# A RetNet recurrence and a PReLU feed-forward block in one kernel: the second half of w_out loaded as fp32 by SyncE's queue and cast on chip, and unit 3 turned by a transposing DMA transfer

## The chip, the cores and the metric

The kernel runs on one core of a Trainium2 chip. The metric is the device time of one launch in microseconds (us). Five engines work beside each other, each in the order of its own list of instructions: TensorE (PE in the profile, with its weight loads as PEld), VectorE (DVE), ScalarE (ACT), GpSimd (POOL) and SyncE (SP, SPq for its DMA queue). Semaphores join them. DMA transfers are issued by SyncE, ScalarE or GpSimd.

## The reference

```python
def _attn_ref(q, k, v):                       # q, k, v: 4 x 8 x 768 x 64
    gamma = 1.0 - 2.0 ** (-5.0 - np.arange(H))
    for t in range(S):
        state = gamma * state + einsum('bhd,bhe->bhde', k[:, :, t], v[:, :, t])
        y[:, :, t] = scale * einsum('bhd,bhde->bhe', q[:, :, t], state)

def _moe_ref(x, w_in, w_out, alpha):          # 3072 x 512, 512 x 2048, 2048 x 512
    h = x @ w_in
    g = np.maximum(h, 0.0) + alpha * np.minimum(h, 0.0)
    return g @ w_out
```

The recurrence's y, with its heads side by side, is x of the second function. All inputs and the output are fp32; the kernel multiplies in fp16 and sums in fp32.

## The kernel before

Each of the four sequences is cut into three units of 256 tokens, so there are units 0 to 11, and two units make a block of 512 tokens for the feed-forward part: blocks 0 to 5. The recurrence is computed in chunks: per unit, scores of q against k under a mask, times v, plus q times the state that is carried on.

For each unit the program does the following. `load` brings k, q and v as fp32 by SyncE's queue (L165, and L159 from unit 4 on, where k and v come in four pieces each); the tiles are ks, qs and vs, with three buffers of each. `rescale` (L185) multiplies k and q by powers of gamma into the fp16 tile kdq; `cast_v` (L201) makes the fp16 tile vx. Then kdq has to be turned, 16 blocks of 128x128, into kq, which has the head dimension on the partitions. For units 0 to 3 `turn_pe` does that on TensorE in two calls of eight transposes into a PSUM bank (trb, L230), each followed by a copy on ScalarE (kq<-trb, L236). From unit 4 on `turn_dma` (L205) does it in one transposing DMA transfer from SBUF to SBUF. `score_mm` (sca and scb, L466) reads kq, `masks` follows on VectorE, `sum_mm` (st, L260) sums the state from kdq and vx, `state_sum` and `state_copy` carry it on, `out_mm` (y, L501, L515 and L533) makes the unit's output, and `take_y` (xT, L556) brings it to SBUF in fp16.

The feed-forward part of a block is `ffn1` (hps, L632; the PReLU with hm on ScalarE, L648, and gt on VectorE, L650) and then the product with w_out: `ffn2` for block 0 (ops, L809, evicted by ScalarE, L819), and from block 1 on `ffn2_seven`, which forms seven products where eight would be needed, from sums of quarters of g and of w_out (ox, oy, L857). The sums of w_out's quarters, wsum, are made once by `w_sums` (L572): the first on GpSimd from w_out's first half alone, three on VectorE, which read the second half too.

The order of everything is written out by hand. `ffn1` and `ffn2` are generators; `tick(gen, m)` puts the next m matmuls of one into TensorE's list, so that the unit's small products stand between them. Around unit 3, `gen` is `ffn2` of block 0 (64 matmuls of 512 columns, in four groups of 16; a group reads four of w_out's 16 row tiles), and `half` is `ffn1` of block 1, of which 48 matmuls need only unit 2. The banks in which these 48 are summed are given by a list, six turns of eight matmuls.

Weights are brought as fp32 and cast to fp16 on chip: `get_wo32(i)` loads part i of w_out, two row tiles (512 KB), into space that is free early, and `cast_wo` casts it on the engine that is given. That holds for parts 0 to 3. The second half comes by `get_wo` (L982), a DMA transfer that GpSimd issues and that casts on its way, in two transfers of four row tiles. The second piece of the loads of unit 4, its q, waits for the first of these two, by `held`.

SyncE's queue is one list: a transfer whose condition isn't met stands in the way of all behind it.

Of the kernel before, what the change touches and what calls it, by code (L numbers as in the profile page):

```python
# [9 lines left out]
FP = mybir.dt.float32  # L10
# [12 lines left out]
def kernel(  # L23
# [10 lines left out]
    nc = tc.nc  # L34
    B, H, S, D = q.shape
# [41 lines left out]
    sbp = ctx.enter_context(tc.tile_pool(name="sbp", bufs=1, space=bass.MemoryType.SB))  # L77
# [38 lines left out]
    held, late, last_g = [], [], []  # L116
# [26 lines left out]
    def load(u, parts="kqv"):  # L143
        if u >= NU:
            return
        b, c = divmod(u, UPB)
        t = staged.setdefault(u, {})
        for nm in parts:
            src = {"k": k, "q": q, "v": v}[nm[0]]
            if nm[0] not in t:  # L150
                t[nm[0]] = sbp.tile(
                    [128, H, 2 * D], FP, tag=f"{nm[0]}s", bufs=3, name=f"{nm[0]}s{u}"
                )
            h = slice(0, H) if len(nm) == 1 else slice(4 * int(nm[1]), 4 * int(nm[1]) + 4)
            if u >= SPLIT and nm != "q":
                for x in range(2):
                    for y in range(2):
                        at = U * c + 128 * x + 64 * y
                        nc.sync.dma_start(  # L159
                            out=t[nm][rows(x), :, D * y : D * y + D],  # L160
                            in_=src[b, :, at : at + 64, :].rearrange("h p d -> p h d"),
                        )
                continue
            hold(
                nc.sync.dma_start(  # L165
                    out=t[nm[0]][:, h, :],
                    in_=src[b, h, U * c : U * c + U, :].rearrange(
                        "h (p r) d -> p h (r d)", r=2
                    ),
                )  # L170
            )
# [10 lines left out]
    def rescale(eng, u, t, h0, h1):  # L182
        kdq = unit(u)[0]
        at = OQ if t else (O2 if u >= SPLIT else 0)
        return eng.tensor_tensor(  # L185
            out=kdq[:, t, :, h0:h1, :].rearrange("p r h d -> p h r d"),
            in0=staged[u]["kq"[t]][:, h0:h1, :].rearrange("p h (r d) -> p h r d", r=2),
            in1=tab[:, at + 2 * h0 : at + 2 * h1]
            .rearrange("p (h r) -> p h r", r=2)
            .unsqueeze(3)  # L190
            .to_broadcast([128, h1 - h0, 2, D]),
            op=MULT,
        )

    def cast_v(eng, u, h0=0, h1=H):
        o = unit(u)[2][:, h0:h1].rearrange("p h r d -> p (h r d)")
        i = staged[u]["v"][:, h0:h1].rearrange("p h x -> p (h x)")
        if eng is nc.scalar:
            eng.activation(out=o, in_=i, func=COPY, bias=0.0, scale=1.0)
        else:  # L200
            eng.tensor_copy(out=o, in_=i)  # L201

    def turn_dma(u):
        kdq, kq, _ = unit(u)
        nc.sync.dma_start_transpose(out=kq, in_=kdq.rearrange("p t r h d -> p (t r h d)"))  # L205
# [410 lines left out]
    def ffn1(n, banks, apart=0):  # L616


        turns = [(f, 2, ul, ul + 1) for ul in range(2) for f in range(0, apart, 2)]
        rest = range(apart, NFT)  # L620
        if apart == 0:
            rest = [f + x for f in range(HF) for x in (0, HF)]
        turns += [(f, 1, 0, 2) for f in rest]
        gt = None
        for i, (f0, nf, lo, hi) in enumerate(turns):
            hps = ps(banks[i % len(banks)], "hps").rearrange("p (f t) -> p f t", f=nf)
            parts = [(f, lo, hi) for f in range(nf)]
            if n > 1 and i == 0:
                parts = [(0, 0, 1), (0, 1, 2)]
            for f, ul, uh in parts:  # L630
                for hp in range(4):
                    nc.tensor.matmul(  # L632
                        out=hps[:, f, U * (ul - lo) : U * (uh - lo)].rearrange(
                            "p (u t) -> p u t", t=U
                        ),
                        lhsT=w_in_all[:, hp, 128 * (f0 + f) : 128 * (f0 + f) + 128],
                        rhs=xT[n][:, ul:uh, hp, :],
                        start=(hp == 0),
                        stop=(hp == 3),
                    )  # L640
                    if (f, ul, uh) != parts[-1] or hp < 3:
                        yield
            if gt is None:
                gt = sbp.tile([128, NFT, TB], F16, tag="gt", bufs=2, name=f"gt{n}")
                gts[n] = gt
            hm = sbp.tile([128, TB], FP, tag="hm", bufs=3, name="hm")
            hm = hm.rearrange("p (f t) -> p f t", f=nf)
            nc.scalar.activation(out=hm, in_=hps, func=RELU, bias=0.0, scale=-1.0)  # L648
            for f in range(nf):
                nc.vector.scalar_tensor_tensor(  # L650
                    out=gt[:, f0 + f, U * lo : U * hi],
                    in0=hm[:, f, :],
                    scalar=oma_sb[:, f0 + f : f0 + f + 1],
                    in1=hps[:, f, :],
                    op0=MULT,
                    op1=ADD,
                )
            if n > 0 and f0 in ((HF + 3, NFT - 1) if apart == 0 else (NFT - 1,)):

                lo = 0 if apart or f0 < NFT - 1 else 4  # L660
                hi = HF if f0 == NFT - 1 else 4
                g_sums(n, 0, lo, hi)
                g_sums(n, 1, lo, hi)
            yield
# [294 lines left out]
    def tick(gen, m=10**6):  # L959
        for _ in range(m):  # L960
            if next(gen, 1) == 1:
                return
# [14 lines left out]
            return eng.activation(out=o, in_=i, func=COPY, bias=0.0, scale=1.0)  # L977
        return eng.tensor_copy(out=o, in_=i)  # L978

    def get_wo(i):  # L980
        s = slice(4 * i, 4 * i + 4)
        return nc.gpsimd.dma_start(out=w_out_all[:, s, :], in_=wo[:, s, :])  # L982

    def wo_part(i):
        return early[i // 2][:, 1, 2 * (i % 2) : 2 * (i % 2) + 2, :]

    def get_wo32(i):
        nc.sync.dma_start(out=wo_part(i), in_=wo[:, 2 * i : 2 * i + 2, :])
# [113 lines left out]
    rescale(G, 2, 1, 4, 8)  # L1102
    cast_wo(G, 3)
    load(3, ("k", "q", "v"))
    cast_v(G, 2)
    out_mm(1, (4, 5), evict=False)
    take_y(1, (0,))
# [2 lines left out]


    gen = ffn2(0, (0, 1, 2, 3), parts=4)
    half = ffn1(1, (6, 7, 4, 5, 4, 6, 0, 1, 2, 3, 0, 4, 5, 6, 7, 1), apart=12)
    tick(gen, 8)
    turn_pe(2, 0, 5)
    tick(gen, 6)
# [7 lines left out]
    sum_mm(2, (5, 4))  # L1124
    state(2, 0, G, "ga")
    masks(2, 1)
    held.append(get_wo(2))
    load(4)
    load(5)
    rescale(G, 3, 0, 0, 8)  # L1130
    rescale(G, 3, 1, 0, 8)
    get_wo(3)
    cast_v(G, 3)
    w_sums(0, 0, HF, G)
    tick(gen, 7)
    out_mm(2, (4, 5))
    tick(gen, 6)
    tick(half, 24)
    turn_pe(3, 0, 6)
    tick(half, 8)  # L1140
    turn_pe(3, 1, 7)
    tick(half, 16)
    tick(gen, 9)
    score_mm(3, 0, (4, 5))
    masks(3, 0)
# [192 lines left out]
```

## Time and profile before

| | us |
|---|---|
| median of 3 runs | 198.63 (198.36 to 198.85) |
| the profiled execution | 198.86 |
| its span | 196.9 |
| TensorE busy in the span | 189.3 |
| VectorE, ScalarE, GpSimd busy | 156.3, 115.4, 106.1 |

The span runs from the first to the last instruction of the profiled execution, and the profile's times count from its start. The chain of work that ended last is followed back from the last instruction, at each step to what released it. A row of the timeline has start, length, engine, line, operation and tiles, and in brackets the idle time ahead of it and what ended it. A group's row has its busy time and the mean of one in ns. The granted clock of TensorE was 0.997 of full speed over the span.

### The profile page before, as it was taken

The numbers are of one execution on the slowest core, as the hardware profiler recorded it, in microseconds if no ns is written. First come the engines' busy times: TensorE is split into PE (matmuls) and PEld (weight loads), VectorE is DVE, ScalarE is ACT, GpSimd is POOL, SyncE is SP. The second block draws the span as 40 slices with busy tenths as digits, with TensorE's granted clock in tenths as the row PEclk, the third lists the DMA queues.
The fourth block names the chain that finished last, engine by engine and source line by source line (L and its number), as shares of the span: only waits on it lengthen the run. The fifth ranks groups of instructions, "written<-read, shape, count | busy, mean of one in ns | idle before, by whom it ended". The sixth has DMA issues, their size and how long they took to land.

```text
span 196.9 us, 6085 instructions
## 1 busy us (share of the span) xinstructions
PE 189.3 (96%) x2529; PEld 128.8 (65%) x2529; DVE 156.3 (79%) x259; ACT 115.4 (59%) x199; POOL 106.1 (54%) x113
## 2 busy tenths in 40 slices
PE   6688999999999999999999999999999999999993
PEld 2356645568467688744688744788644788865882
DVE  7698987517698998289988389977489996999983
ACT  4458665349187668467467476467466486678110
POOL 3176897499549544970077980076970180039300
PEclk9999999999999999999999999999999999999998
DMA  5999999998879989898988899929865010400014
GB/s 156 313 317 380 374 381 377 293 180 136 211 192 200 286 197 265 213 311 175 213 203 209 256 201 191 222 65 225 256 122 126 17 57 3 160 3 0 0 65 152
DMA packets 90026, 37.92 MB, mean 193 GB/s; under 512 B 57984, under 2 KB 87696, under 8 KB 90000
## 3 DMA queue, kind: packets, MB, share of 16 engines
q1 hardware_dynamic: 88768, 36.45, 69.2%
q0 software_dynamic: 1056, 1.05, 3.6%
q8 instruction: 20, 0.33, 0.6%
q10 hardware_dynamic: 176, 0.04, 0.1%
q14 instruction: 6, 0.05, 0.1%
HBM read 27.31 MB, written 6.29 MB: 171 GB/s over the span
## 4 chain that ended last, share of the span: by engine, by line
PE 90%; SPq 4%; DMA 3%; DVE 0%; issue 0%; POOL 0%; DVEq 0%
PE hps L632 36%; PE ox L857 16%; PE oy L857 12%; PE ops L809 7%; SPq L165 4%; PE hps L719 4%; PE sp L761 3%; DMA vs<-in_v_dram 3%; PE y L533 1%; PE y L384 1%; PE trb L230 1%; PE st L284 1%; PE sca L466 1%; PE ov L857 1%; PE ow L857 1%; PE oz L857 1%
## 5 line engine op out<-in xcount | busy, mean ns | idle before, releaser
L632 PE MATMUL hps<-xT,win 128*128 128x512 f16 (+1 forms) x396 | 71.5, 338 | 0.3 <-DVE ss L423 0.3
L650 DVE SCALAR_TENSOR_TENSOR gt<-hm,oma,hps 128x512 f16<-128x512 f32 (+1 forms) x96 | 59.4, 656 | 12.1 <-issue 4.3
L648 ACT ACTIVATE hm<-hps 128x512 f32<-128x512 f32 x80 | 47.6, 597 | 24.6 <-PE hps L632 22.5
L632 PEld LDWEIGHTS <-win 128*128 128x128 f16 x396 | 38.1, 98 | 31.0 <-POOL win L978 0.4
L857 PEld LDWEIGHTS <-gs 128*128 128x128 f16 x320 | 31.0, 98 | 3.7
L857 PEld LDWEIGHTS <-gt 128*128 128x128 f16 x240 | 22.9, 98 | 4.0
L333 POOL CAST tg<-tm 64x256 f16<-64x256 f32 x12 | 4.8, 396 | 34.3 <-DVE tm L301 22.3
L185 POOL TENSOR_TENSOR kdq<-qs,tab 128x1024 f16<-128x1024 f32 (+1 forms) x12 | 20.2, 1686 | 3.0 <-DVE wsum L572 2.3
L185 POOL TENSOR_TENSOR kdq<-ks,tab 128x1024 f16<-128x1024 f32 (+1 forms) x12 | 20.2, 1686 | 2.6 <-PE y L515 2.6
L857 PE MATMUL ox<-wout,gt 128*128 128x256 f16 x144 | 17.3, 273 | 0.0
L857 PE MATMUL oy<-wsum,gs 128*128 128x256 f16 x144 | 17.2, 273 | 0.0
L556 ACT ACTIVATE xT<-y 128x512 f16<-128x512 f32 x22 | 14.9, 744 | 3.1 <-PE y L533 2.0
L201 POOL CAST vx<-vs 128x1024 f16<-128x1024 f32 (+1 forms) x13 | 12.6, 970 | 6.7 <-DMA vs<-in_v_dram 6.7
L809 PE MATMUL ops<-wout,gt 128*128 128x512 f16 x64 | 15.3, 380 | 0.0
L613 DVE TENSOR_TENSOR gs<-gt 128x1024 f16<-128x1024 f16 (+1 forms) x14 | 13.0, 934 | 0.2
L877 ACT ACTIVATE cu<-oy 128x512 f32<-128x512 f32 x10 | 6.0, 597 | 10.6 <-PE oy L857 10.1
L236 ACT ACTIVATE kq<-trb 128x1024 f16<-128x1024 f16 x8 | 8.2, 1023 | 6.3 <-PE trb L230 6.3
L313 POOL TENSOR_TENSOR tf<-ss,tab 128x256 f32<-128x256 f32 x10 | 10.3, 1028 | 2.5 <-DVE ss L312 1.3
L881 DVE TENSOR_TENSOR os<-ox,cu 128x512 f32<-128x512 f32 x5 | 3.4, 687 | 10.1 <-PE ox L857 10.1
L670 POOL TENSOR_SCALAR hn<-qc,oma 128x256 f32<-128x256 f32 x4 | 4.5, 1138 | 12.4 <-DVE qc L785 12.3
L809 PEld LDWEIGHTS <-gt 128*128 128x128 f16 x64 | 5.8, 98 | 6.0
L424 POOL TENSOR_TENSOR tf<-ss,tab 128x256 f32<-128x256 f32 x6 | 5.9, 980 | 7.1 <-DVE ss L423 7.1
(119 smaller groups left out, 293.1 us busy)
## 6 DMA issues: line engine op xcount, KB each, us to landing
qs<-in_q_dram SPq DMA_DIRECT2D x9, 512.0 KB, 5.4
ks<-in_k_dram SPq DMA_DIRECT2D x32, 128.0 KB, 3.5
vs<-in_v_dram SPq DMA_DIRECT2D x32, 128.0 KB, 4.6
early<-in_moe_w_in_dram SPq DMA_DIRECT2D x7, 512.0 KB, 7.5
out_dram<-os SPq DMA_DIRECT2D x9, 256.0 KB, 2.5
early<-in_moe_w_out_dram SPq DMA_DIRECT2D x4, 512.0 KB, 7.0
out_dram<-ot SPq DMA_DIRECT2D x4, 512.0 KB, 3.8
ks<-in_k_dram SPq DMA_DIRECT2D x6, 256.0 KB, 6.1
```

What stands on the lines that cost most here:

```text
L165: nc.sync.dma_start(out=t[nm[0]][:, h, :], in_=src[b, h, U * c : U * c + U, :].rearrange("h (p r) d -> p h (r d)", r=2),)
L185: return eng.tensor_tensor(out=kdq[:, t, :, h0:h1, :].rearrange("p r h d -> p h r d"), in0=staged[u]["kq"[t]][:, h0:h1, :].rearrange("p h ...
L201: eng.tensor_copy(out=o, in_=i)
L236: nc.scalar.activation(out=kq.rearrange("p (x a) i -> p x a i", x=4)[:, :, 2 * hh : 2 * hh + 2, :], in_=trb.rearrange("p (x a i) -> p x a ...
L313: nc.gpsimd.tensor_tensor(out=t, in0=ss, in1=dec, op=MULT)
L556: nc.scalar.activation(out=o, in_=i, func=COPY, bias=0.0, scale=1.0,)
L613: last_g.append(nc.vector.tensor_tensor(out=o, in0=a, in1=b, op=op))
L632: nc.tensor.matmul(out=hps[:, f, U * (ul - lo) : U * (uh - lo)].rearrange("p (u t) -> p u t", t=U), lhsT=w_in_all[:, hp, 128 * (f0 + f) : ...
L648: nc.scalar.activation(out=hm, in_=hps, func=RELU, bias=0.0, scale=-1.0)
L650: nc.vector.scalar_tensor_tensor(out=gt[:, f0 + f, U * lo : U * hi], in0=hm[:, f, :], scalar=oma_sb[:, f0 + f : f0 + f + 1], in1=hps[:, f, :],
L809: nc.tensor.matmul(out=opss[tq], lhsT=gt[:, ft, 128 * tq : 128 * tq + 128], rhs=w_out_all[:, ft, :], start=(ft == 0), stop=(ft == NFT - 1),)
L857: nc.tensor.matmul(out=o[1][m], lhsT=lhs(f, m), rhs=rhs(f), start=(first and f == 0 and (m == 0 or o[0] is None)), stop=(f == HF - 1), ski ...
```

## The change

The two transfers by GpSimd's queue are gone, and with them the hold on unit 4's loads. w_out's parts 4 to 7 are loaded as fp32 by SyncE's queue into free buffers of the tags ks, qs, vs and ks: parts 4 and 5 right behind unit 3's loads, parts 6 and 7 behind the transposing transfer of unit 3. Part 5 is cast on GpSimd, parts 4, 6 and 7 on ScalarE. Unit 3's 16 transposes on TensorE and their two copies on ScalarE are gone; `turn_dma(3)` takes their place, behind unit 3's rescales. The loads of units 4 and 5 stand behind all that. The 48 matmuls of block 1 follow each other without a break, and their fifth and sixth turn are summed in banks 6 and 7 instead of 4 and 6.

```diff
@@ -977,12 +977,16 @@
             return eng.activation(out=o, in_=i, func=COPY, bias=0.0, scale=1.0)
         return eng.tensor_copy(out=o, in_=i)
 
-    def get_wo(i):
-        s = slice(4 * i, 4 * i + 4)
-        return nc.gpsimd.dma_start(out=w_out_all[:, s, :], in_=wo[:, s, :])
+    wo_parts = {}
 
     def wo_part(i):
-        return early[i // 2][:, 1, 2 * (i % 2) : 2 * (i % 2) + 2, :]
+        if i < 4:
+            return early[i // 2][:, 1, 2 * (i % 2) : 2 * (i % 2) + 2, :]
+        if i not in wo_parts:
+            tag = ("ks", "qs", "vs", "ks")[i - 4]
+            t = sbp.tile([128, H, 2 * D], FP, tag=tag, bufs=3, name=f"wo{i}")
+            wo_parts[i] = t.rearrange("p h x -> p (h x)").rearrange("p (f d) -> p f d", f=2)
+        return wo_parts[i]
 
     def get_wo32(i):
         nc.sync.dma_start(out=wo_part(i), in_=wo[:, 2 * i : 2 * i + 2, :])
@@ -1102,6 +1106,8 @@
     rescale(G, 2, 1, 4, 8)
     cast_wo(G, 3)
     load(3, ("k", "q", "v"))
+    get_wo32(4)
+    get_wo32(5)
     cast_v(G, 2)
     out_mm(1, (4, 5), evict=False)
     take_y(1, (0,))
@@ -1110,7 +1116,7 @@
 
 
     gen = ffn2(0, (0, 1, 2, 3), parts=4)
-    half = ffn1(1, (6, 7, 4, 5, 4, 6, 0, 1, 2, 3, 0, 4, 5, 6, 7, 1), apart=12)
+    half = ffn1(1, (6, 7, 4, 5, 6, 7, 0, 1, 2, 3, 0, 4, 5, 6, 7, 1), apart=12)
     tick(gen, 8)
     turn_pe(2, 0, 5)
     tick(gen, 6)
@@ -1124,22 +1130,23 @@
     sum_mm(2, (5, 4))
     state(2, 0, G, "ga")
     masks(2, 1)
-    held.append(get_wo(2))
+    rescale(G, 3, 0, 0, 8)
+    rescale(G, 3, 1, 0, 8)
+    turn_dma(3)
+    get_wo32(6)
+    get_wo32(7)
+    cast_wo(G, 5)
+    cast_v(G, 3)
     load(4)
     load(5)
-    rescale(G, 3, 0, 0, 8)
-    rescale(G, 3, 1, 0, 8)
-    get_wo(3)
-    cast_v(G, 3)
     w_sums(0, 0, HF, G)
     tick(gen, 7)
     out_mm(2, (4, 5))
+    cast_wo(A, 4)
     tick(gen, 6)
-    tick(half, 24)
-    turn_pe(3, 0, 6)
-    tick(half, 8)
-    turn_pe(3, 1, 7)
-    tick(half, 16)
+    tick(half, 48)
+    cast_wo(A, 6)
+    cast_wo(A, 7)
     tick(gen, 9)
     score_mm(3, 0, (4, 5))
     masks(3, 0)
```

SyncE's queue ahead of unit 4, before (ks, qs and vs are unit 3's in the first three rows, then unit 4's and unit 5's):

```order
L165 DMA ks_456<-in_k_dram 128x8x128
L165 DMA qs_458<-in_q_dram 128x8x128
L165 DMA vs_460<-in_v_dram 128x8x128
L159 DMA ks_762<-in_k_dram 64x8x64 x4
L165 DMA qs_767<-in_q_dram 128x8x128
L159 DMA vs_769<-in_v_dram 64x8x64 x4
L159 DMA ks_774<-in_k_dram 64x8x64 x4
L165 DMA qs_779<-in_q_dram 128x8x128
L159 DMA vs_781<-in_v_dram 64x8x64 x4
L205 DMA_TRANSPOSE kq_1021<-kdq_1020 128x16x128
```

and in the changed kernel, from unit 3's v on (wo are the four parts of w_out):

```order
L165 DMA vs_460<-in_v_dram 128x8x128
L992 DMA wo_462<-in_moe_w_out_dram 128x2x512
L992 DMA wo_464<-in_moe_w_out_dram 128x2x512
L205 DMA_TRANSPOSE kq_766<-kdq_765 128x16x128
L992 DMA wo_771<-in_moe_w_out_dram 128x2x512
L992 DMA wo_773<-in_moe_w_out_dram 128x2x512
L159 DMA ks_777<-in_k_dram 64x8x64 x4
L165 DMA qs_782<-in_q_dram 128x8x128
L159 DMA vs_784<-in_v_dram 64x8x64 x4
L159 DMA ks_789<-in_k_dram 64x8x64 x4
L165 DMA qs_794<-in_q_dram 128x8x128
L159 DMA vs_796<-in_v_dram 64x8x64 x4
```

Two parts, unit 3's transposition and two more parts have moved in ahead of unit 4's k.

ScalarE's list behind unit 2's output (xT), before:

```order
L556 ACTIVATE xT_843<-y_802 128x4x2x64
L648 ACTIVATE hm<-hps 128x512 x3
L236 ACTIVATE kq_787<-trb 128x4x256
L648 ACTIVATE hm<-hps 128x512
L236 ACTIVATE kq_787<-trb 128x4x256
L648 ACTIVATE hm<-hps 128x512 x2
L450 ACTIVATE tg<-tf_0_1016 64x4x64
```

and in the changed kernel:

```order
L556 ACTIVATE xT_851<-y_809 128x4x2x64
L997 ACTIVATE wout<-wo_462 128x1024
L648 ACTIVATE hm<-hps 128x512 x6
L997 ACTIVATE wout<-wo_771 128x1024
L997 ACTIVATE wout<-wo_773 128x1024
L450 ACTIVATE tg<-tf_0_1007 64x4x64
```

The two copies of kq are gone, and the casts of parts 4, 6 and 7 stand around the six hm.

## The prediction

> **What bounds the kernel now.** I read the page's busy times first, then the chain of work that ended last, in order of time, around unit 3.
>
> ```profile
> PE 189.3 (96%) x2529; PEld 128.8 (65%) x2529; DVE 156.3 (79%) x259; ACT 115.4 (59%) x199; POOL 106.1 (54%) x113
> DMA  5999999998879989898988899929865010400014
> ```
>
> TensorE is busy for 96% of the span, so time can be won here almost only by taking work off TensorE, and lost only by making it wait. The second line says that the DMA engines have little room until the 29th of the 40 slices (4.92 us each): a transfer that is added or put later may collide.
>
> ```profile
> 44.95 0.60 PE trb L230 x8
> 45.55 0.87 PE hps L632 x8
> 46.43 0.45 PE trb L230 x8
> 46.87 1.75 PE hps L632 x16
> 48.62 1.94 PE ops L809 x9
> 50.56 0.17 PE sca L466
> ...
> 51.19 1.83 PE ops L809 x8
> ...
> 53.37 1.83 PE ops L809 x8
> ...
> 68.19 0.56 PE st L260 x44
> ...
> 74.33 0.05 PE sca L466 x2
> ```
>
> Columns: start, length, what. In this stretch the chain is TensorE without a break. The two trb pieces are unit 3's transposes; they are on the chain and nothing covers them. The rest gives the dates by which the new suppliers must deliver: sca at 50.56 is the first reader of unit 3's turned tile kq.
>
> **The change part by part.** (a) Removed from TensorE: the two trb pieces, 0.60 + 0.45 = **1.05 us**, all on the chain. Every later date of TensorE moves forward by as much, as long as nobody is late: unit 3's scores begin at 50.56 - 1.05 = 49.5. The 9 ops at 48.62 are numbers 33 to 41 of block 0's 64 (32 stand ahead of the half of block 1), and those at 51.19 numbers 42 to 49. Number 49 is the first to read part 6 of w_out (parts have two of the 16 row tiles), at 51.19 + 7 x 0.23 - 1.05 = 51.75. Number 51 is the first to read part 7, at 53.37 + 0.23 - 1.05 = 52.55.
>
> (b) The transposing transfer. It needs unit 3's kdq, which GpSimd makes.
>
> ```profile
> 39.61 0.99 POOL L982 DMA_DIRECT2D wout<-in_moe_w_out_dram  x1
> ...
> 42.49 1.91 POOL L185 TENSOR_TENSOR kdq<-qs,tab 128x1024 f16<-128x1024 f32 x1
> 44.34 0.81 POOL L982 DMA_DIRECT2D wout<-in_moe_w_out_dram  x1
> 45.15 1.05 POOL L201 CAST vx<-vs 128x1024 f16<-128x1024 f32 x1
> ...
> 58.93 1.90 POOL L185 TENSOR_TENSOR kdq<-qs,tab 128x1024 f16<-128x1024 f32 x1 [2.30 <-DVE wsum L572]
> ...
> 62.64 2.02 POOL L201 CAST vx<-vs 128x1024 f16<-128x1024 f32 x2
> 64.62 1.90 POOL L185 TENSOR_TENSOR kdq<-qs,tab 128x1024 f16<-128x1024 f32 x1
> ```
>
> GpSimd loses the two DMA issues (0.99 + 0.81) and gains one cast (1.05, like vx). So the second rescale ends near 44.40 - 0.99 = 43.4, and SyncE issues the transposition there. The nearest rows for its landing are the eight that the kernel already has:
>
> ```profile
> kq<-kdq SPq DMA_TRANSPOSE x8, 4.8
> early<-in_moe_w_out_dram SPq DMA_DIRECT2D x4, 512.0 KB, 7.0
> ...
> 60.86 1.79 SPq L205 DMA_TRANSPOSE kq<-kdq  x1
> ...
> DMA to landing us min/median/max: 5.4/5.4/5.4
> ...
> DMA to landing us min/median/max: 4.2/4.2/4.2
> ```
>
> From issue to landing the median is 4.8 us; line L205 alone gives 5.4 for one early in the span and 4.2 for one late. I take 4.8, the same shape in the same queue: landed at 48.2. With 5.4 it is 48.8, with 4.2 47.6, with the 7.0 us of loads in a full queue 50.4. The scores ask at 49.5, so by the rows of its own kind TensorE waits for nothing and 0.7 to 1.9 us are to spare; at the far end it waits 0.9. The other end: no more can be gained here than the 1.05 and the 0.17 us in which sca starts.
>
> The Trainium skill, page "VectorE: DVE Perf Modes", section "Rules for kernel authors", speaks against this edit: for a 128x128 transpose it says to use TensorE where PSUM will do, and the DMA crossbar otherwise; its section "The three transpose paths" has 390 ns on TensorE against 1309 ns by DMA. Taken one after the other, 16 blocks by that price would be an estimated 20.9 us, landing at 64 and leaving TensorE waiting some 15 us. The trace disagrees: a transposition of 16 such blocks landed in 4.2 to 5.4 us, and what counts here is whose time it is, not how long one block takes.
>
> (c) w_out's second half. Parts 4 and 5 are issued behind unit 3's loads, in the place of unit 4's k.
>
> ```profile
> 28.00:30.00 2.00, 2.00 (x11) 0.93 (x10) 1.65 (x4) 1.35 (x3) 1.94 (x3) 1.00 1.12 368
> ...
> 42.00:44.00 2.00, 1.98 (x18) 1.64 (x17) 0.07 (x1) 0.72 (x2) 2.00 (x2) 1.00 1.14 164
> ...
> 33.84 1.39 SPq L165 DMA_DIRECT2D vs<-in_v_dram  x1
> 35.33 4.33 SPq L159 DMA_DIRECT2D ks<-in_k_dram  x4
> 46.50 0.38 SPq L165 DMA_DIRECT2D qs<-in_q_dram  x1
> ...
> 56.35 3.53 SPq L159 DMA_DIRECT2D vs<-in_v_dram  x4
> ...
> ks<-in_k_dram SPq DMA_DIRECT2D x32, 128.0 KB, 3.5
> vs<-in_v_dram SPq DMA_DIRECT2D x32, 128.0 KB, 4.6
> ```
>
> The last columns of the two windows are DMA share and GB/s. At 368 GB/s, 512 KB takes 1.42 us; while GpSimd's casting transfers run, full engines move only 164. A whole tile takes SyncE 0.38 (q) to 1.39 us (v) to issue; I take 0.7. Issued at 35.3 and 36.0, with the 7.0 us of the first loads of w_out, which met a full queue as these do, parts 4 and 5 land by 42.3 and 43.0. ScalarE casts part 4 ahead of block 1's hm, and parts 6 and 7 behind the sixth:
>
> ```profile
> 40.78 1.34 ACT L556 ACTIVATE xT<-y 128x512 f16<-128x512 f32 x2 [1.14 <-PE y L533]
> 43.24 0.60 ACT L648 ACTIVATE hm<-hps 128x512 f32<-128x512 f32 x1 [1.12 <-PE hps L632]
> ...
> L236 ACT ACTIVATE kq<-trb 128x1024 f16<-128x1024 f16 x8 | 8.2, 1023 | 6.3 <-PE trb L230 6.3
> ...
> L977 ACT ACTIVATE win<-early x2: 630/630/630, 16.2 to 17.5; 128x512 f16<-128x512 f32 x2
> ```
>
> A cast of 128x1024 on ScalarE isn't in the trace; between kq at 1.02 and twice win at 1.26 I take 1.05, nearest the row of its size. The idle 1.12 us at 42.12 to 43.24 hides part 4's cast but for the 0.1 to 0.2 us by which it may start late, and the hm at 0.60 each catch that up, as TensorE makes one each 0.87 (hps x8). Part 5's cast stands on GpSimd at 43.4 and is wanted by number 35 at 48: hidden. ScalarE loses two kq evictions (2.05) and gains three casts (3.15); that is off the chain while the dates hold.
>
> Parts 6 and 7 are the tight ones, since SyncE issues them behind the transposition: 43.4 + 1.8 = 45.2, and 45.9. Nothing else is left in the queue by then, as parts 4 and 5 are done, so I add 1.42 us for each to the landing of the transposition: 49.6 and 51.0. Casts end near 50.7 and 52.1 against 51.75 and 52.55: spare time 1.0 and 0.45 us. The far end is the 7.0 us of w_out's first loads: 52.2 and 52.9, casts to 53.3 and 54.3, and TensorE waits 1.55 for part 6 and 0.2 more for part 7. I take the lower end, because the 7.0 was measured in a queue full since the start of the program, and this one is emptied by its wait for GpSimd.
>
> (d) Units 4 and 5's loads move back. k of unit 4 is issued after the parts, near 46.6 instead of 35.3, and needed by GpSimd at about 52 (its rescale follows a state copy that TensorE sets). Four k pieces at 0.88 (a quarter of the v row at 56.35) and 3.5 to landing are there near 53: GpSimd loses about a microsecond there, and gets it back, since the next rescale waits 2.30 us for VectorE's wsum at 58.93. The v pieces of unit 5 end at 59.9 before; the total ahead of them is the parts and the transposition more, the slow casting transfers less, so I put them at 60 to 61. Unit 4's transposition, issued at 61, lands by 66.4 and is wanted right after st, at 67.7. The last v piece, issued at 60.1 and 4.6 to landing, is there at 64.7, and unit 5's vx 1.0 later at 65.7 (64.66 before), wanted by st at 68.19 - 1.05 = 67.1. Unit 5's second rescale follows (66.52 before, now 67.6), and its transposition lands 4.8 to 5.4 later, 72.4 to 73.0, wanted at 74.33 - 1.05 = 73.3. All are in time, the last by 0.3 us at the least.
>
> Sum: -1.05, and nothing added. The profiled execution took 198.86 (span 196.9, 1.96 outside), which gives 197.8; the median of the runs shown is 198.63, 0.23 less, so I forecast **197.6**.
>
> **Rivals.** *Parts 6 and 7 come late* (slower): the chain becomes transposition, load, cast, ops. By the 7.0 us row TensorE waits 1.75 us: 198.63 - 1.05 + 1.75 = 199.3. It decides from a wait of 1.65 us on (1.05 and 0.6, which is 0.3%). For it: the digits 8 and 7 of the DMA line between 44 and 54 us, and 0.45 us to spare. Against: GpSimd's slow transfers, which make up much of those digits, are gone.
>
> *The transposition comes late*: its price is one for one from 49.5 on. It wipes out the gain to within 0.3% if it lands 0.45 to 1.65 us late, 50.0 to 51.1, 6.6 to 7.7 us after its issue; beyond that the kernel is slower. For it: 7.0 us would leave it 0.9 late, 198.5. Against: the medians of its own kind.
>
> *Units 4 and 5 late*: if unit 5's v goes out 2 us later than put above, unit 4's transposition, behind it in SyncE's queue, lands 0.7 us past its date: 198.3. At 3 us it makes the kernel slower, at 4 us 200.3. For it: the queue issues no two steps at a time. Against: GpSimd's transfers no longer slow it.
>
> *The gain is swallowed by VectorE*, which runs 8 us without a break in the second part of block 1:
>
> ```profile
> 59.83 8.03 DVE L650 SCALAR_TENSOR_TENSOR gt<-hm,oma,hps 128x256 f16<-128x256 f32 x16 [0.97 <-ACT hm L648]
> ```
>
> Then nothing changes, 198.6. Against: it idles 0.97 us for ScalarE's hm, and so for TensorE, before it starts, and would start earlier too.
>
> **Chances.** Forecast as said, 197.2 to 198.0: 0.62. Transposition late, or swallowed (within 0.3%, about what a measurement of this kernel can tell): 0.15. Parts late enough, 0.16, and units 4 and 5 late, 0.07: slower. Range 197.2 (0.17 more gain and 0.2 of scatter) to 199.3, the late parts.
>
> **What would show it.** TensorE's chain without trb between 42 and 48, nine ops from 47.6 and sca at 49.5 with no wait on DMA; ScalarE's two casts ended before 52.5; unit 4's transposition issued near 61; the span 1.0 shorter. I am wrong if ops waits for the cast of part 6 or 7, or sca for the transposition, or if SyncE's queue issues unit 4's k much after 47.

## The result: 0.6% slower, and where the time went

The changed kernel takes 199.83 us in the median of 19 runs (198.92 to 201.75); the kernel before took 198.60 in the 19 runs beside them. The ratio is 1.0062 with a 95% interval of 1.0039 to 1.0086. The forecast was 197.6. The profiled execution after took 200.95 us (span 199.1), 1.1 more than its median, and a second profile, below, loses in the same stages. Medians are of all runs, while the ratios leave out runs of more than 1.5% above a kernel's shortest: none here, and below the three longest of ten and the four longest of 13 with unit 4's k first, the two longest of ten with a spare load in the kernel before, and one run each with two buffers os, with unit 3 turned by both, and with unit 4's k and part 6 first.

The page after, engines first, then the load of the DMA engines in 40 slices of the span:

```profile
PE 189.9 (95%) x2513; PEld 128.3 (64%) x2513; DVE 158.4 (80%) x259; ACT 116.7 (59%) x200; POOL 105.6 (53%) x112
DMA  5999999949989798899797998998866110400014
```

TensorE has the 16 transposes fewer, but its busy time has not fallen. The new 4 in the ninth slice is a hole of some two microseconds in which the DMA engines do next to nothing.

The chain of waits before, three rows: the first hps of block 1's second part, of block 2 and of block 3.

```profile
57.75 8.69 PE hps L632 x64
...
78.10 0.54 PE hps L632 x4
...
107.06 0.54 PE hps L632 x4
```

The same chain after, with what stands in it around these places:

```profile
45.62 6.46 DMA wo<-in_moe_w_out_dram
...
52.11 1.06 ACT wout L997
...
53.21 1.67 PE ops L809 x7
...
57.30 8.71 PE hps L632 x64
...
67.44 1.77 DVE gs L613
...
78.72 0.54 PE hps L632 x4
...
103.93 4.23 DMA qf<-kq
...
109.23 0.54 PE hps L632 x4
```

At 57.30 the kernel is 0.45 us ahead of before. At 78.72 it is 0.62 behind, at 109.23 it is 2.17 behind, and that stays to the end (span +2.2). TensorE is no longer the whole chain: a load of w_out, VectorE, and a small transfer (qf) stand in it.

SyncE's queue after, the steps around the change (start, length of the issue):

```profile
35.41 2.34 SPq L992 DMA_DIRECT2D wo<-in_moe_w_out_dram  x2
43.20 1.73 SPq L205 DMA_TRANSPOSE kq<-kdq  x1
44.99 1.12 SPq L992 DMA_DIRECT2D wo<-in_moe_w_out_dram  x2
46.15 3.10 SPq L159 DMA_DIRECT2D ks<-in_k_dram  x4
...
61.87 2.98 SPq L205 DMA_TRANSPOSE kq<-kdq  x1
64.95 0.99 SPq L1174 DMA_DIRECT2D out_dram<-os  x2
...
69.54 2.17 SPq L205 DMA_TRANSPOSE kq<-kdq  x1
```

and the queue before, unit 5's transposition:

```profile
66.61 2.07 SPq L205 DMA_TRANSPOSE kq<-kdq  x1
```

Waits after that the kernel before did not have, with the total, the number and the longest in us, and one stretch of two microseconds (last columns: DMA share and GB/s):

```profile
SPq L205 <- POOL wout L998: 6.3, 1, 6.3
...
DVE os L881 <- DMA out_dram<-os: 5.1, 1, 5.1
POOL kdq L185 <- DMA ks<-in_k_dram: 3.5, 2, 1.9
...
ACT qf L218 <- DMA kq<-kdq: 1.2, 1, 1.2
...
PE ops L809 <- ACT wout L997: 0.8, 1, 0.8
PE y L384 <- DMA qf<-kq: 0.7, 1, 0.7
```

```profile
42.00:44.00 2.00, 2.00 (x19) 1.80 (x19) 0.28 (x1) 1.68 (x3) 2.00 (x2) 1.00 0.02 6
```

SyncE's list stands for 5.4 us at unit 3's transposition, from 37.75 to 43.20, waiting for GpSimd's rescales, the second of which ended at 43.17. (The row of the waits has 6.3, since it counts on to the end of the cast behind them.) Meanwhile the DMA engines run dry: 6 GB/s where the kernel before had 164. What is behind in the list comes late: unit 5's transposition is issued at 69.54 instead of 66.61. Unit 3's own transposition did no harm: sca began at 49.2 without a wait on it.

In stage 2 TensorE's late dates come from two places, which the rows above only touch: VectorE's sums of quarters of g (gs, L613), which take longer beside a late operation of GpSimd, and ScalarE's move of unit 5's q (qf, L218), which waits for the late transposition. Unit 5's second rescale on GpSimd after, then the first sum of block 1 before and after:

```profile
66.21 1.90 POOL L185 TENSOR_TENSOR kdq<-qs,tab 128x1024 f16<-128x1024 f32 x1
```

```profile
67.89 1.23 DVE L613 TENSOR_TENSOR gs<-gt 128x2048 f16<-128x2048 f16 x1
```

```profile
67.44 1.76 DVE L613 TENSOR_TENSOR gs<-gt 128x2048 f16<-128x2048 f16 x1
```

Before, that rescale began at 64.62 and was over ahead of the sums.

For the experiments the span is cut at four marks of TensorE's timeline: the first y on L533 after 39 us, and the first hps of block 1's second part, of block 2 and of block 3. The table has the length of each stage in one profiled execution, as the difference to before (17.47, 20.45 and 28.96 us). The columns gs have how much longer than before VectorE's first two sums of a block's g took together: block 1's in stage 2 (2.46 us before), block 2's in stage 3 (1.38). Behind the last mark none of them differs by more than 0.24, but for the one with a load more (0.55).

| kernel | begins | stage 1, to 57.6 | stage 2, to 78.0 | gs in 2 | stage 3, to 107.0 | gs in 3 |
|---|---|---|---|---|---|---|
| changed | -0.21 | -0.24 | +1.08 | +0.52 | +1.54 | +0.31 |
| changed, second profile | -0.09 | -0.34 | +0.78 | +0.79 | +2.11 | +1.37 |
| TensorE turns unit 3 | +0.06 | +0.85 | 0.00 | 0.00 | +0.46 | +0.37 |
| transposition alone | -0.20 | +6.81 | +0.10 | 0.00 | 0.00 | 0.00 |
| both turn unit 3 | -0.90 | +0.01 | +2.05 | +0.96 | +0.10 | 0.00 |
| parts 6, 7 first | +0.09 | **-1.04** | +1.08 | +0.15 | +0.91 | +0.80 |
| the same, two buffers os | +0.23 | -0.91 | +2.42 | +2.43 | +0.78 | +0.29 |
| one load more | +0.02 | -1.03 | +3.61 | +0.82 | +1.25 | +0.96 |
| no parts 6, 7 | -0.26 | -0.46 | 0.00 | -0.01 | +0.30 | 0.00 |
| spare load, kernel before | +1.58 | +0.01 | 0.00 | 0.00 | +2.23 | +1.05 |
| unit 4's k first | -0.32 | **-1.04** | 0.00 | -0.01 | +0.04 | 0.00 |
| unit 4's k first, again | +0.80 | +1.28 | +0.73 | -0.01 | +0.97 | +0.87 |
| unit 4's k and part 6 first | -0.33 | +0.15 | -0.01 | 0.00 | +1.09 | +1.03 |
| unit 5's transposition first | -0.12 | +0.73 | +1.68 | +1.09 | +1.89 | +1.50 |

One profile stands for one run only: the two of the changed kernel differ by 0.57 us in stage 3, and the two with unit 4's k first by 2.32 in stage 1.

### The profile page after: what moved, and what is told of

Same layout as the page of the kernel before. It is cut to its first block, busy times and chain, and to the rows that moved or that the text cites. A ratio compares the mean times of both kernels' runs of the same rounds, so it can differ in the third digit from the quotient of the medians.

```text
span 199.1 us, 6057 instructions
## 1 busy us (share of the span) xinstructions
PE 189.9 (95%) x2513; PEld 128.3 (64%) x2513; DVE 158.4 (80%) x259; ACT 116.7 (59%) x200; POOL 105.6 (53%) x112
## 4 chain that ended last, share of the span: by engine, by line
PE 68%; SPq 11%; DMA 8%; POOL 4%; ACT 3%; issue 2%; DVE 2%; POOLq 0%
PE hps L632 30%; PE ox L857 11%; PE oy L857 9%; SPq L165 5%; PE ops L809 4%; PE hps L719 3%; DMA wo<-in_moe_w_out_dram 3%; PE sp L761 3%; SPq L159 3%; DMA early<-in_moe_w_in_dram 3%; SPq L205 3%; DMA qf<-kq 2%; POOL kdq L185 2%; PE y L384 1%; PE y L533 1%
## 5 line engine op out<-in xcount | busy, mean ns | idle before, releaser
L650 DVE SCALAR_TENSOR_TENSOR gt<-hm,oma,hps 128x512 f16<-128x512 f32 (+1 forms) x96 | 58.8, 655 | 9.2 <-POOL kdq L185 4.3
L613 DVE TENSOR_TENSOR gs<-gt 128x1024 f16<-128x1024 f16 (+1 forms) x14 | 13.8, 993 | 0.2
L313 POOL TENSOR_TENSOR tf<-ss,tab 128x256 f32<-128x256 f32 x10 | 10.3, 1028 | 2.5 <-DVE ss L312 1.3
L236 ACT ACTIVATE kq<-trb 128x1024 f16<-128x1024 f16 x6 | 6.1, 1023 | 6.3 <-PE trb L230 6.2
L450 ACT ACTIVATE th<-tf 64x256 f16<-64x256 f32 x15 | 6.2, 415 | 4.6 <-POOL tf L313 2.4
```

The lines of the kernel that those rows point to most:

```text
L313: nc.gpsimd.tensor_tensor(out=t, in0=ss, in1=dec, op=MULT)
L450: nc.scalar.activation(out=o, in_=i, func=COPY, bias=0.0, scale=1.0)
L613: last_g.append(nc.vector.tensor_tensor(out=o, in0=a, in1=b, op=op))
L650: nc.vector.scalar_tensor_tensor(out=gt[:, f0 + f, U * lo : U * hi], in0=hm[:, f, :], scalar=oma_sb[:, f0 + f : f0 + f + 1], in1=hps[:, f, :],
```

## The experiments

The theory after the result was that of a debt: the standing still (put at 6.3 us) and a transposition more make SyncE's queue late, and until 107 us it has no room to catch up. Its rivals put the loss into single waits or into on-chip work.

**Each part alone.** First w_out's parts by SyncE, with unit 3 turned by TensorE as before (the list of banks goes back too):

```diff
...
-    turn_dma(3)
...
-    tick(half, 48)
+    tick(half, 24)
+    turn_pe(3, 0, 6)
+    tick(half, 8)
+    turn_pe(3, 1, 7)
+    tick(half, 16)
```

> The changed kernel with one part undone: unit 3 is turned by TensorE again, w_out's second half still comes as fp32 by SyncE's queue. Theory Q (queue debt: SyncE's list stands 6.3 us for unit 3's rescales ahead of the transposing transfer, the DMA engines are idle at 42 to 44 us, and the transfer itself takes 2 us more, so that the loads of units 4 to 7 and all behind them come about 3 us late): the wait and the transfer are gone, TensorE has its 1.05 us back, so the time is near that of before, 198.2 to 198.9. Theory P (the fp32 parts are the cost: part 7's cast ends too late, and the casts load ScalarE): the parts still come by the same queue, so the time stays over that of before by more than 0.6 us, 199.3 or more.

Measured: 199.62 us, ratio 1.0048 (1.0011 to 1.0084), outside both expectations on the side of the rival. The fp32 parts cost something without any transposition. In its profile it is at one place in the main, part 4, on ScalarE's timeline (in brackets the idle time ahead and what ended it):

```profile
43.20 1.06 ACT L997 ACTIVATE wout<-wo 128x1024 f16<-128x1024 f32 x1 [1.01 <-DMA wo<-in_moe_w_out_dram]
```

ScalarE waited 1.01 us for the load, with block 1's hm behind the cast, and TensorE's trb came 0.84 us later than it could. The page puts that wait down to GpSimd's cast of part 5, which waited 1.32 us for its load and ended within 0.1 us of the hm; which of the two held TensorE isn't settled. Parts 4 and 5 are issued ahead of everything that this edit touches, so their late landing is scatter that the changed kernel can meet too. Stage 2 is untouched.

Then the transposition alone, in the kernel before, between unit 4's k and the rest of its loads:

```diff
-    load(4)
-    load(5)
+    load(4, "k")
     rescale(G, 3, 0, 0, 8)
     rescale(G, 3, 1, 0, 8)
+    turn_dma(3)
     get_wo(3)
+    load(4, "qv")
+    load(5)
...
-    tick(half, 24)
-    turn_pe(3, 0, 6)
-    tick(half, 8)
-    turn_pe(3, 1, 7)
-    tick(half, 16)
+    tick(half, 48)
```

> The kernel before with the other part alone: unit 3 is turned by the transposing transfer, which stands in SyncE's list between unit 4's k and q, where that list waits for GpSimd's first casting transfer anyway; w_out's second half comes by GpSimd's queue as before. Theory Q: the transfer is put where the list stands still, so nearly all of TensorE's 1.05 us is won: 197.5 to 198.2. If a transposing transfer costs by itself, in whatever place, by 2 us of DMA time on a queue that has no slack up to 110 us, the gain is eaten: 198.6 to 199.8. Theory P: no fp32 parts, so the whole 1.05 us is won, 197.6.

Measured: 203.98 us, ratio 1.0272 (1.0215 to 1.0329). Neither expectation had it. The chain of that kernel:

```profile
44.23 10.81 DMA kq<-kdq
55.09 0.31 PE sca L466
...
56.16 3.48 PE ops L809 x8
```

Beside GpSimd's casting transfers the transposition took 10.81 us to land instead of 4.2 to 5.4, and TensorE waited 5.5 us. The two parts of the change belong together: beside GpSimd's transfers the transposition doesn't pay at this place.

**The order in SyncE's queue.** Parts 6 and 7 ahead of the transposition, so that the idle microseconds are used:

```diff
+    get_wo32(6)
+    get_wo32(7)
     turn_dma(3)
-    get_wo32(6)
-    get_wo32(7)
```

> The changed kernel with parts 6 and 7 issued ahead of the transposing transfer, right behind parts 4 and 5, so that they move while SyncE's list waits for unit 3's rescales. Theory Q: the idle 2 to 3 us of the DMA engines at 42 to 44 are used, so units 4 and 5 come as much earlier; the time falls from 199.83 by 1 to 2 us, to 197.9 to 198.8. Theory P: only the 0.8 us in which TensorE waits for part 7's cast is saved, 199.0.

Measured: 200.51 us, ratio 1.0090 (1.0056 to 1.0124); neither. But the first stage shows the predicted gain whole, in TensorE's rows of the chain:

```profile
56.80 8.69 PE hps L632 x64
...
78.23 0.54 PE hps L632 x4
...
108.10 0.54 PE hps L632 x4
```

56.80 is 0.95 ahead of before. By 78.23 it is gone, by 108.10 another 0.91 is lost. Unit 5's transposition is issued at 68.28, VectorE waits 4.41 us for the store of os. So the late dates of stages 2 and 3 don't need part 7's wait. Stage 3's loss is for the most part VectorE's: block 2's second sum, before, and in this run with GpSimd's cast of unit 7's v beside it:

```profile
90.79 0.69 DVE L613 TENSOR_TENSOR gs<-gs,gt 128x1024 f16<-128x1024 f16 x1
```

```profile
90.36 1.50 POOL L201 CAST vx<-vs 128x1024 f16<-128x1024 f32 x1
```

```profile
91.00 1.41 DVE L613 TENSOR_TENSOR gs<-gs,gt 128x1024 f16<-128x1024 f16 x1
```

Would the store's wait be the loss in stage 3? The same kernel with a second buffer for os:

```diff
-    OUTS = {"os": 1, "cu": 3}
+    OUTS = {"os": 2, "cu": 3}
```

> The kernel with parts 6 and 7 ahead of the transposition, and with two buffers instead of one for the output tile os, so that VectorE need not wait for the late store of that tile (4.41 us at 83.0 there). Theory (late steps of SyncE's queue cost time at each place where an engine needs them): TensorE's loss between 82 and 108 us goes from 0.9 to 0.2 or less, 199.4 to 199.9 against 200.5 with one buffer. Rival (the wait for the store stands in front of work that would have waited anyway, for the next units' loads): within 0.3 of 200.5.

Measured: 200.05 us, ratio 1.0054 (1.0020 to 1.0088), between the two ranges. The wait for the store is gone, and stage 3 still loses 0.78. Here the theory's reading of that wait fell: it stands in front of other late work. In stage 2 this run lost 2.42, all of it (2.43) in the sums of g, as unit 5's last rescale came at 68.18.

**The amount of work in the queue.** One spare load of 512 KB behind part 7, read by nobody:

```diff
     get_wo32(7)
+    spare = sbp.tile([128, H, 2 * D], FP, tag="qs", bufs=3, name="spare")
+    nc.sync.dma_start(
+        out=spare.rearrange("p h x -> p (h x)").rearrange("p (f d) -> p f d", f=2),
+        in_=wo[:, 0:2, :],
+    )
```

> The changed kernel with one more load of 512 KB (part 0 of w_out into a buffer that nobody reads) behind part 7 in SyncE's list, ahead of unit 4's k: 1.4 us of DMA time more, nothing else. Theory Q: all that is behind moves back by 1.4 us, and the time grows by 0.7 to 1.5 us, to 200.5 to 201.3. Theory P: it stands behind part 7 and changes nothing, 199.8.

Measured: 203.19 us, ratio 1.0215 (1.0178 to 1.0252). The direction is the theory's, the size more than expected: by the ratios 3.0 us more than the changed kernel, for a load that takes 1.4 us at full rate.

Less work: without the transfers of parts 6 and 7.

```diff
     turn_dma(3)
-    get_wo32(6)
-    get_wo32(7)
...
         if i < 4:
             return early[i // 2][:, 1, 2 * (i % 2) : 2 * (i % 2) + 2, :]
+        i = 4 + i % 2
```

> The changed kernel without the transfers of parts 6 and 7 of w_out: the casts read parts 4 and 5 a second time, so those rows of w_out are wrong in the product. 1 MB less in SyncE's queue, the transposition stays. Theory (the total of work in SyncE's queue is what makes everything behind it late): the loads of units 4 and 5 come about 2 us earlier, no wait for the cast of part 7, 197.5 to 198.5. Rival (the wait of SyncE's queue for GpSimd's rescales with the transposition behind it is what costs, whatever stands after it): 199.0 to 199.8.

The casts of parts 6 and 7 read parts 4 and 5 a second time, so the product leaves out a quarter of w_out. Measured: 198.39 us, ratio 0.9969 (0.9933 to 1.0005), in the theory's range. With 1 MB less in the queue stage 2 loses nothing and stage 3 0.30, though SyncE's list stands nearly as long for the rescales (5.1 us). So the standing alone isn't the loss; it is what has to go through the queue after it. In stage 1 part 4 was late here (ScalarE waited 1.55 us for it, and TensorE 0.41 for the hm behind its cast), so the gain was 0.46 only.

And the same spare load in the kernel before:

```diff
     load(4)
+    spare = sbp.tile([128, H, 2 * D], FP, tag="qs", bufs=3, name="spare")
+    nc.sync.dma_start(
...
     load(5)
```

> The kernel before with one spare load of 512 KB between unit 4's and unit 5's loads, read by nothing. Theory (the queue has no slack between 45 and 110 us in either kernel): 1.4 us or more of lateness reach unit 5's transposition and the stores, 199.5 to 202.0. Rival (the kernel before has slack there, and only the changed order used it up): 198.5 to 199.0.

Measured: 198.90 us, ratio 1.0004 (0.9969 to 1.0040). The rival was right: in most runs the kernel before had room for it. Not in all, though: two of the ten took 201.24 and 202.73, where the longest of the 31 beside them without the load took 200.59. The profile fell on the longest; it began 1.58 us late, ahead of the load, and lost 2.23 in stage 3. By the ratios the same load costs 0.0% before and 1.5% after: the change used up the room.

**Unit 4's k into the hole.**

```diff
+    load(4, "k")
     rescale(G, 3, 0, 0, 8)
     rescale(G, 3, 1, 0, 8)
     turn_dma(3)
...
-    load(4)
+    load(4, "qv")
```

> The changed kernel with unit 4's k issued ahead of the transposition, so that it fills the microseconds in which the DMA engines were idle. Theory (idle DMA time in the wait is the debt): GpSimd's wait of 1.89 for that k and the slow VectorE sums beside its late rescale go, unit 5's transposition starts 1 to 2 us earlier, 198.7 to 199.4. Rival (the order within the queue is worth nothing, only its total): 199.6 to 200.0.

Measured: ten runs from 197.55 to 202.49 us, median 200.06, just above the rival's range; ratio 1.0006 (0.9960 to 1.0052). The profile shows one of the short ones, and in it the forecast gain comes out at every place (TensorE's chain, then SyncE's queue):

```profile
56.38 8.69 PE hps L632 x64
...
76.74 0.54 PE hps L632 x4
...
105.74 0.54 PE hps L632 x4
```

```profile
66.22 2.22 SPq L205 DMA_TRANSPOSE kq<-kdq  x1
```

Unit 5's transposition is issued 0.39 us earlier than before, stages 2 and 3 lose nothing, the span is 195.7 against 196.9. Since the runs fell into two groups, the same kernel once more:

> The kernel with unit 4's k ahead of the transposition once more, unchanged, since its ten runs fell into 197.5 to 197.8 (three) and 199.7 to 202.5 (seven), and its profile shows one of the first. Theory (one order of instructions, and the landing of single transfers decides in each run whether dates with half a microsecond to spare hold): both groups again; a profile of the upper group has the same work on SyncE's queue, with TensorE losing at unit 3's or unit 5's transposition, the stores or qf of unit 7. Rival (the first group is the kernel's time and the others are disturbed at random places of the program): losses spread over places that have nothing to do with SyncE's queue.

Measured: 13 runs from 197.43 to 202.67 us, median 199.12; ratio 0.9963 (0.9935 to 0.9991). Of the 23 runs of both, 8 lie at 198.16 or below and 11 at 199.71 or above; their median is 199.30. This time the profile fell on the longest run. Unit 3's transposition in SyncE's queue, then TensorE's timeline with its waits in brackets:

```profile
44.21 4.26 SPq L205 DMA_TRANSPOSE kq<-kdq  x1
```

```profile
51.20 0.24 PE L466 MATMUL sca<-kq 64*64 64x128 f16 x1 [0.88 <-DMA kq<-kdq]
54.48 0.38 PE L809 MATMUL ops<-wout,gt 128*128 128x512 f16 x1 [0.96 <-ACT wout L997]
55.74 1.67 PE L809 MATMUL ops<-wout,gt 128*128 128x512 f16 x7 [0.22 <-ACT wout L997]
```

The same program, 5.1 us apart. 1.12 of it are there at the first mark: SyncE's issues of w_in's nine loads, long ahead of the change, took 10.45 us instead of 9.26. Stage 1 takes 2.32 more: the transposition met a full queue and came 0.88 late, which put parts 6 and 7 behind it late by 0.96 and 0.22. Stages 2 and 3 take 0.73 and 0.93 more, by the move of unit 5's q and by stretched sums of g (0.87). Every one of these places hangs on SyncE's queue, the last by way of GpSimd, whose inputs come late.

A middle way, unit 4's k and part 6 ahead of the transposition and part 7 behind:

```diff
+    load(4, "k")
+    get_wo32(6)
     rescale(G, 3, 0, 0, 8)
     rescale(G, 3, 1, 0, 8)
     turn_dma(3)
-    get_wo32(6)
     get_wo32(7)
...
-    load(4)
+    load(4, "qv")
```

> The changed kernel with unit 4's k and part 6 ahead of the transposition and part 7 behind it: no idle time of the DMA engines in the wait, and part 7 alone left to come in time. Theory (SyncE's queue in its order is what costs; filled, the predicted gain of about 1 us comes out): 197.4 to 198.6. Rival (the order within the queue moves the loss but doesn't remove it, since the DMA engines are busy for 95% of the first 110 us and the kernel gives them more to do): 199.2 to 200.2.

Measured: 200.18 us, ratio 1.0044 (1.0011 to 1.0076): the rival's. The transposition's time to landing, changed kernel first, then this one:

```profile
DMA to landing us min/median/max: 3.7/3.7/3.7
```

```profile
DMA to landing us min/median/max: 6.2/6.2/6.2
```

Behind the hole it lands in 3.7 us, behind a full queue in 6.2 (6.1 in the kernel with two buffers of os), and then TensorE waits for it (1.1 us here). Filling the hole doesn't always make the transposition late: with parts 6 and 7 ahead of it, with and without the second os, and in the short run with unit 4's k ahead, sca did not wait. With two buffers os it landed 0.05 us ahead of sca.

Unit 5's transposition ahead of the six late stores:

```diff
     turn_dma(4)
+    turn_dma(5)
     for i, (o, t) in enumerate(late):
...
-    turn_dma(5)
```

> The changed kernel with unit 5's transposition ahead of the six late stores in SyncE's queue. Theory (that transposition, 2.9 us later than before, is where TensorE loses 1 us by 78.7): 199.0 to 199.5, with the loss between 67 and 78 us halved or gone. Rival (the stores come later by as much, and VectorE's wait for the store of os, 5.07 us in the changed kernel, takes it back by 108): 199.6 to 200.2.

Measured: 202.09 us, ratio 1.0153 (1.0115 to 1.0191). Worse than both ranges. Part 7 was later here than in the changed kernel (TensorE waited 1.7 us for its cast), which the edit doesn't explain. Behind that, SyncE's list now stood until 69.76 for unit 5's second rescale (ended at 69.74) with the stores behind it, and ScalarE got the tile os at 74.23 instead of 72.01, when its store had landed.

**A second profile of the change, and the price of the transposition.** The changed kernel again, unchanged:

> The changed kernel once more, unchanged, for a second profile: the first one took 200.95 us, and the median of its runs is 199.83. Theory (the dates that fail differ from run to run, since each has half a microsecond to spare or less, and the time is the sum of those that failed): a run near the median has TensorE's loss at only one or two of the four places (part 7's cast 0.8, unit 5's transposition by 78.7, the store of os, qf of unit 7). Rival (a fixed loss): all four again, with the same sizes.

Measured: 201.06 us in four runs (200.38 to 202.72), ratio 1.0138 (1.0079 to 1.0197), span 199.5. Neither came out: the losses are in the same stages, of the same order, but not at the same operations. Part 7's cast holds TensorE again (stage 1 -0.34). Stage 2's 0.78 is here the stretched sum of g alone (2.02 us), where the first profile had that (1.76) and the move of unit 5's q. Stage 3 loses 2.11, with the wait for the store of os in the chain and two stretched sums behind it (2.75 us instead of 1.38), where the first profile had qf of unit 7:

```profile
79.16 5.32 DMA out_dram<-os
```

The same program has the ratio 1.0062 in the 19 runs made first and 1.0138 in these four, made later, with intervals that just touch. So totals measured at different times don't rank kernels that lie within 0.8% of each other, and against these four runs the load more costs 0.8% only. Clear of it are the transposition alone (slower), and the kernel without parts 6 and 7 and the second set of runs with unit 4's k first (faster); for the rest the stages are the evidence.

Last, unit 3 turned by both, the transfer into a spare tile that nobody reads:

```diff
-    turn_dma(3)
+    spare = sbp.tile([128, 4 * NP, 128], F16, tag="spare", bufs=1, name="spare")
+    nc.sync.dma_start_transpose(
...
-    tick(half, 48)
+    tick(half, 24)
+    turn_pe(3, 0, 6)
...
```

> The changed kernel with unit 3 turned by TensorE as before, and the transposing transfer still issued at its place, into a spare tile that nobody reads. Against the kernel with TensorE alone (199.62) it shows what the transposition costs those behind it in SyncE's queue. Theory (its 2 us of waiting and issuing and its time on the DMA engines make units 4 to 7 later, which is what ate the 1.05 us it saves): 200.4 to 201.4. Rival (the fp32 parts alone make the queue late, and the transposition is carried along for nothing): 199.4 to 199.9.

Measured: 200.66 us, ratio 1.0088 (1.0058 to 1.0118), in the theory's range. But what the transposition costs those behind it isn't shown. Against TensorE alone (1.0048) it is some 0.4% by the ratios, whose intervals overlap and which were measured at different times; measured together with this kernel, the changed one, without TensorE's transposes, was no faster (1.0138). And the profile, which loses 2.05 in stage 2, began 0.90 early: up to the last mark it is 1.26 behind the kernel before, and TensorE alone is 1.37 behind.

## Why the prediction was wrong, point by point

- **(a), the 1.05 us: right.** Stage 1 is 1.04 shorter wherever nobody is late (parts 6, 7 first; unit 4's k first). VectorE swallowed none of it there.
- **(b), the transposition: right.** Issued at 43.20 against 43.4, it landed in 3.7 us, under the 4.2 of the shortest row quoted, since the queue had run dry, as (c) says of it. Behind a full queue it is 6.1 to 7.0, near the 6.6 from which the rival has it wipe out the gain.
- **(c), part 7: a term mis-sized.** "Nothing else is left in the queue by then, as parts 4 and 5 are done, so I add 1.42 us for each to the landing of the transposition": part 6 did land by 49.08 (forecast 49.6), but part 7 at 52.1 instead of 51.0. Its cast ended at 53.17 instead of 52.1, past the date 52.55, and TensorE waited 0.8. Unit 4's k was issued right behind the parts and may have shared the engines with part 7, but that isn't shown: with one load more just as close behind it, part 7 landed by 51.2. The spare 0.45 was less than the uncertainty of one load. So the rival *parts 6 and 7 late* (0.16) had this place right.
- **(d) is the step that failed**: "All are in time, the last by 0.3 us at the least". Unit 4's k came as forecast (issued at 46.15, GpSimd's rescale began at 53.66 after a wait of 1.89). Then three things were not in the sum.
  - GpSimd did not get the microsecond back for nothing. Its late operations now ran beside VectorE's sums: of w_out first (last section), and then unit 5's second rescale, at 66.21, beside the first sum of g. That is about half of the 1.08 that stage 2 lost, and all of it in the second profile.
  - The queue between unit 4's and unit 5's transpositions was not walked. Unit 4's was issued at 61.87, slowly (2.98), and landed at 68.31, just ahead of its reader; the six late stores ran until 69.4, and unit 5's went out at 69.54 where 67.6 was put.
  - The date for unit 5's tile was that of TensorE's scores (73.3), but ScalarE's move of its q (qf) reads the same tile ahead of them: it began at 72.56 before, so 71.5 by the forecast, while the landing was put at 72.4 to 73.0. After, qf waited 1.17 us, until 73.8, and that is the other half of stage 2's loss.
- **Behind 74 us the working had nothing**, and stage 3 lost 1.54. Units 6 and 7 go through the same queue, later by the same debt. In every kernel that loses more than 0.30 in stage 3, block 2's sums of g are stretched there by a late operation of GpSimd for unit 7 (column gs in 3); where they are not, it loses 0.30 or less. The run of the kernel before with a spare load shows that its queue has room for about one 512 KB load in most runs; the change took more.
- Of the rivals, *units 4 and 5 late* (0.07) had the main place right, and priced 2 us of lateness at 198.3, as though it ended with unit 4's transposition.

What is left open: how much of stage 3 in the first profile of the changed kernel (1.54, of which the sums are 0.31) is qf of unit 7 and how much what stands ahead of it in SyncE's list, what made part 7 late, and why the first 20 us vary by over a microsecond from run to run. That a late operation of GpSimd stretches the sums is read from the traces; no kernel was run only to keep the two apart. No order tried beats the kernel before in the median of all its runs.

## What to carry to other kernels

Before work is moved to a queue that the DMA line shows at 8 and 9 for most of the span, walk everything behind it to the end of that stretch, stores and later units too, and not to the first reader alone: here a load of 512 KB cost nothing in most runs before the change and 1.5 to 3.0 us after it. Take the date of a tile from its first reader on any engine, and look at what a late operation will then run beside. A step that waits for an engine stops the whole list; filling the hole ahead of it can make that step itself late. And dates kept by 0.3 to 0.45 us, where single transfers vary by 1 to 3 us, should be counted as missed about as often as kept.

## What the runs showed of the hardware that was not expected

The time of a transposing transfer depends on its company: 3.7 us behind an idle queue, 6.1 to 7.0 behind a full one, 10.81 beside GpSimd's casting transfers (one run).

VectorE's operations on two tiles stretch beside GpSimd's. Rows of the timelines: VectorE's first sum of w_out before, then GpSimd's late rescale and the same sum after.

```profile
54.95 1.22 DVE L572 TENSOR_TENSOR wsum<-wout,wsum 128x2048 f16<-128x2048 f16 x1
```

```profile
53.66 1.90 POOL L185 TENSOR_TENSOR kdq<-ks,tab 128x1024 f16<-128x1024 f32 x1 [1.89 <-DMA ks<-in_k_dram]
```

```profile
53.69 2.95 DVE L572 TENSOR_TENSOR wsum<-wout,wsum 128x2048 f16<-128x2048 f16 x1
```

2.95 instead of 1.22 us, and the rescale, which began 0.03 us earlier, took no longer than elsewhere. The Trainium skill, page "SBUF — State Buffer", section "SBUF: two separate sides", says that the port pair they share is locked for a whole instruction by whichever starts first; the trace agrees, as 1.22 and the rescale's remaining 1.87 make 3.09. The sum of g at 67.44 fits as well: 1.23 and the remaining 0.67 of the rescale at 66.21 make 1.90, and it took 1.76.

TensorE's clock fell in the long wait of the kernel with the transposition alone. Three stretches of that run (the column ahead of the DMA share is the granted clock):

```profile
52.00:54.00 2.00, 0.00 (x0) 0.00 (x0) 0.00 (x0) 0.00 (x0) 0.00 (x0) 0.66 1.26 230
...
56.00:58.00 2.00, 2.00 (x17) 0.76 (x10) 1.39 (x3) 0.41 (x1) 0.54 (x2) 0.50 1.03 209
...
60.00:62.00 2.00, 2.00 (x12) 0.85 (x12) 1.98 (x4) 0.96 (x2) 0.28 (x1) 1.00 0.97 261
```

The eight ops at 56.16 took 3.48 us instead of 1.83, and stage 1 of that run is 6.81 longer although the 1.05 were saved: the wait of 5.5 cost 7.9. The Trainium skill, page "TensorE: Matmul & The Clock Gate", section "What's actually happening", gives half the clock after an idle window of some 3.4 us, and the full one after as long a busy one; the 0.50 agrees. The waits of the changed kernel, 0.8 and less, left the clock at 1.00.
